# A decode kernel on one core: both FFN layers moved ahead of the attention heads, sums stacked, two engines' loops rolled, the last loads cut finer

## Chip, cores, metric

One core of one Trainium2 chip. The metric is the device time of one execution in microseconds (us), the median of the fast runs. "Span" is the length of the profiled execution as the trace shows it; the measured time of the same execution is 2.0 to 2.4 us longer.

## The reference

One decode step for two batch rows. x is 2x1x512, the caches are 2x32x8192x128 each, all bf16:

```python
xn = layernorm(x)                                     # over 512
q  = (xn @ wq) -> 2 x 32 heads x 128                  # wq 512 x 4096
p  = softmax(q . k_cache * 128**-0.5)                 # 8192 keys a head
o  = (p . v_cache) @ wo                               # wo 4096 x 512
h  = relu(xn @ w1)                                    # w1 512 x 1792
return x + o + h @ w2                                 # w2 1792 x 512
```

K and V are 268 MB of the 280.5 MB read, so this is a streaming kernel: every byte is used once.

## The kernel before

One engine (sync) issues all large loads into one queue. K and V are double buffered in 4.19 MB slots, one slot for one pair of heads (32 pairs). For each pair, TensorE (PE) transposes K in 16 groups of 8, VectorE (DVE) and ScalarE (ACT) copy the groups out of PSUM, PE makes scores, DVE takes the maximum, ACT the exponentials, and PE sums V of the pair before. The order of the loads, and what each waits for:

```python
nc.sync.dma_start(vs[1][:], wq).then_inc(dV[1], 16)      # wq borrows a V slot
block = nc.Block(no_gpsimd_drain=True)                   # (a barrier at its exit)
@block.sync
def _(sp):
    load_k(0); load_k(1); load_v(0)
    for t in range(NP - 1):
        if t + R < NP:
            sp.wait_ge(pT, NG * (t + 1))   # the transposes of pair t are done
            load_k(t + R)
        sp.wait_ge(sW, t + 1)              # the V sums of pair t-1 are done
        load_v(t + 1)
    # x8 (x again), w1, w2, then wo in three cuts (16, 12 and 4 of 32)
    sp.wait_ge(sE, 1)
    sp.dma_start(out, osb).then_inc(dO, 16)
# ... (cut)
block.__exit__(None, None, None)
nc.sync.wait_ge(dO, 16)
```

PE is rolled (a loop of 16 passes, two pairs each); DVE and ACT are straight code of 32 steps. q is 128 small matmuls of 2 columns; FFN1 and FFN2 (56 each) and the output projection (128) come in PE's tail, after the last V:

```python
for h in range(H):
    for kt in range(KT):
        pe.matmul(qp[:, h, :], lhsT=wq_sb[:, kt, h*Dh:(h+1)*Dh], rhs=xnT[:, kt, :], ...)
# ... 16 passes over the pairs, then the last V sums ...
ffn(0, FT // 2)                            # waits for w1
# ... OTn transposes, ffn(FT // 2, FT), selection ...
project(w2_sb, hT, 0, FT, first=True)      # waits for w2
for c in range(3):
    pe.wait_ge(dW[2 + c], 16)              # waits for each cut of wo
    t = project(wo_sb, OX, cuts[c], cuts[c + 1], last=(c == 2))
# then DVE adds x, PE transposes, DVE copies, sync stores
```

## Time and profile before

| | before |
|---|---|
| time, 3 runs | 662.76 us (662.54 to 662.95) |
| span | 660.4 us |
| bytes read | 280.50 MB, mean 425 GB/s |
| last load: first engine done / all 16 done | 652.8 / 656.2 us |
| store issued | 657.6 us |
| store landed, to the end of the span | 1.6 us |

How to read it: the loads are one stream through 16 DMA engines, and a load counts as landed when the last of its 16 has signalled. So the time has four terms: when the first engine is through with all bytes, how far the last engine lies behind it (the *spread*, or lateness), what the compute engines still do after the last landing, and the closing. The prediction shows the lines.

### The profile page before, as it was taken

To read this page: it belongs to the slowest core of one execution; us is meant where nothing else is said; L and a number is where in the kernel's file an instruction comes from. 1 tells how busy PE (TensorE), PEld (TensorE's weight loads), DVE (VectorE), ACT (ScalarE), POOL (GpSimd) and SP (SyncE) were. 2 spreads that over 40 slices of the span, in tenths; PEclk is the share of its full clock that TensorE was granted. 3 is DMA by queue.
4 is the path that set the end of the run, shared out by engine and by line. 5 is a ranking of instruction groups with operands and counts; after the bars stand their busy time and mean duration, and the time that the engine had idled before them with its cause. 6 is when DMAs were issued, how large, how long until landed. Compare 5 with 4: busy or idle time off the path is not lost.

```text
span 660.4 us, 26876 instructions
## 1 busy us (share of the span) xinstructions
PE 551.0 (83%) x12864; PEld 537.0 (81%) x12864; DVE 251.4 (38%) x433; ACT 236.7 (36%) x389; POOL 8.5 (1%) x44
## 2 busy tenths in 40 slices
PE   2577999898887889788798987887997878987976
PEld 2577999888887889788798887887987878987875
DVE  1233544344343434434344443343443433443411
ACT  1242444343433334333243343333343333343410
POOL 1000000000000000000000000000000000000000
PEclk9999999998898999889899898899898989997985
DMA  9999999999999999999999999999999999999995
GB/s 381 416 438 429 424 439 427 437 427 431 437 429 437 427 431 433 429 437 429 431 435 427 439 429 431 435 427 439 427 431 433 429 439 425 435 433 429 437 417 246
DMA packets 10133, 280.73 MB, mean 425 GB/s; under 512 B 1154, under 2 KB 1156, under 8 KB 1284
## 3 DMA queue, kind: packets, MB, share of 16 engines
q1 hardware_dynamic: 10112, 280.50, 98.9%
q8 instruction: 10, 0.16, 0.1%
q14 instruction: 7, 0.06, 0.0%
q10 hardware_dynamic: 4, 0.00, 0.0%
HBM read 280.50 MB, written 0.00 MB: 425 GB/s over the span
## 4 chain that ended last, share of the span: by engine, by line
DMA 62%; PE 34%; ACT 1%; issue 1%; SPq 0%; DVE 0%
DMA ks<-in_A_k_cache_dram 56%; PE tp L233 21%; PE Sc L240 10%; DMA wo_sb<-in_A_wo_dram 5%; PE ot L253 3%; ACT kT L380 1%; PE ot L356 0%; PE Sc L288 0%; PE Sc L291 0%; SPq L171 0%; SPq L168 0%; SPq L166 0%; SPq L149 0%; SPq L167 0%; SPq L147 0%
## 5 line engine op out<-in xcount | busy, mean ns | idle before, releaser
L233 PE MATMUL tp<-identb,ks 128*128 128x128 bf16 x4096 | 324.9, 229 | 77.8 <-DMA ks<-in_A_k_cache_dram 75.9
L380 DVE COPY kT<-tp 128x1024 bf16<-128x1024 bf16 x320 | 219.7, 691 | 332.9 <-PE tp L233 332.7
L233 PEld LDWEIGHTS tp<-identb,ks 128*128 128x128 bf16 x4096 | 256.1, 103 | 81.3 <-DMA ks<-in_A_k_cache_dram 79.1
L380 ACT COPY kT<-tp 128x1024 bf16<-128x1024 bf16 x192 | 194.3, 1012 | 249.6 <-PE tp L233 249.6
L240 PE MATMUL Sc<-q,kT 128*128 128x64 bf16 x4096 | 216.3, 196 | 3.4 <-ACT kT L380 3.4
L240 PEld LDWEIGHTS Sc<-q,kT 128*128 128x128 bf16 x4096 | 178.4, 100 | 6.7 <-ACT kT L380 6.7
L253 PE MATMUL ot<-prm,vs 128*128 128x64 bf16 x4224 | 157.6, 193 | 8.5 <-issue 5.0
L253 PEld LDWEIGHTS ot<-prm,vs 128*128 128x128 bf16 x4224 | 140.5, 98 | 11.4 <-issue 8.8
L483 ACT COPY nm<-Sc 128x2 f32<-128x2 f32 x32 | 5.1, 160 | 118.2 <-PE Sc L291 118.2
L487 ACT ACTIVATE prm<-Sc,nm 64x128 bf16<-64x128 f32 x64 | 25.8, 402 | 1.4
L425 DVE TENSOR_REDUCE mcol<-Sc 64x1 bf16<-64x128 f32 x64 | 18.6, 291 | 17.6 <-PE Sc L240 17.2
L473 ACT COPY OTf<-ot 128x2 f32<-128x2 f32 x33 | 5.3, 160 | 35.3 <-PE ot L253 35.3
L430 DVE TENSOR_REDUCE mx<-Sc 1x2 bf16<-1x128 bf16 x32 | 8.9, 279 | 16.9 <-PE Sc L288 16.9
L203 POOL COPY q<-qb 128x2 bf16<-128x2 bf16 x32 | 5.8, 184 | 582.3 <-PE Sc L240 568.6
L487 ACT ACTIVATION_READ_ACCUMULATOR prm<-Sc,nm 64x1 f32 x64 | 11.8, 185 | 0.0
L218 PE MATMUL ot<-xnT,vs 128*128 128x2 bf16 x128 | 3.6, 165 | 8.3 <-DMA vs<-in_A_wq_dram 8.3
L218 PEld LDWEIGHTS ot<-xnT,vs 128*128 128x128 bf16 x128 | 3.5, 104 | 8.4 <-issue 8.4
L288 PE MATMUL Sc<-identb,mcol 128*1 128x128 bf16 x32 | 7.0, 217 | 0.0
L356 PE MATMUL ot<-OX,wo_sb 128*128 128x2 bf16 x128 | 3.7, 166 | 3.1 <-DMA wo_sb<-in_A_wo_dram 3.1
L356 PEld LDWEIGHTS ot<-OX,wo_sb 128*128 128x128 bf16 x128 | 3.6, 104 | 3.3 <-DMA wo_sb<-in_A_wo_dram 1.9
L291 PE MATMUL Sc<-mx,onesb 1*128 1x2 bf16 x32 | 5.5, 172 | 0.0
L436 DVE CAST xT<-tp 128x8 f32<-128x8 bf16 x1 | 0.2, 166 | 12.5 <-PE Sc L327 12.5
(49 smaller groups left out, 29.4 us busy)
## 6 DMA issues: line engine op xcount, KB each, us to landing
ks<-in_A_k_cache_dram SPq DMA_DIRECT2D x32, 4096.0 KB, 26.8
vs<-in_A_v_cache_dram SPq DMA_DIRECT2D x32, 4096.0 KB, 31.6
vs<-in_A_wq_dram SPq DMA_DIRECT2D x1, 4096.0 KB, 12.2
w_sb<-in_B_w_dram SPq DMA_DIRECT2D x2, 1792.0 KB, 25.9
wo_sb<-in_A_wo_dram SPq DMA_DIRECT2D x1, 2048.0 KB, 32.3
wo_sb<-in_A_wo_dram SPq DMA_DIRECT2D x1, 1536.0 KB, 35.5
wo_sb<-in_A_wo_dram SPq DMA_DIRECT2D x1, 512.0 KB, 36.3
xsb<-in_A_x_dram ACTq DMA_DIRECT2D x1, 2.0 KB
```

The costliest lines, as they stand in the source:

```text
L203: g.tensor_copy(q2[t % R][:], qb[:, 2 * t:2 * t + 2]).then_inc(sQ1, 1)
L218: i = pe.matmul(qp[:, h, :], lhsT=wq_sb[:, kt, h * Dh:(h + 1) * Dh], rhs=xnT[:, kt, :], start=(kt == 0), stop=(kt == KT - 1),)
L233: t = pe.transpose(tp[e % 4][:, i, :], ks[r][:, kk * Dh:(kk + 1) * Dh], identb[:])
L240: t = pe.matmul(Sc[r][:, 2 * kk:2 * kk + 2 * REP], lhsT=kT[e % 4][:, i, :], rhs=rep(q2[r][:]), start=True, stop=True,)
L253: t = pe.matmul(ot[r][:, 0:2 * REP], lhsT=vs[r][:, kk * Dh:(kk + 1) * Dh], rhs=rep(prm[r][:, kk, :]), start=(kk == 0), stop=(kk == KB - 1),)
L288: pe.transpose(tr_of(r), mcol[r][:], identb[:]).then_inc(sT, 1)
L291: pe.matmul(bc_of(r), lhsT=onesb[:], rhs=mx[r][:], start=True, stop=True).then_inc(sB, 1)
L356: t = pe.matmul(fin[:, c, :], lhsT=w[:, j, c * P:(c + 1) * P], rhs=act[:, j, :], start=(first and j == j0 and c == 0), stop=(last and j == ...
L380: fn(kT[e % 4][:], tp[e % 4][:]).then_inc(kR[e], 1)
L425: m = v.tensor_reduce(out=mcol[i][half, :], in_=S_of(i)[half, :, u], axis=AX.X, op=ALU.max)
L430: v.tensor_reduce(out=mx[i][:], in_=tr_of(i).rearrange("o (u m) -> o u m", u=2), axis=AX.X, op=ALU.max, negate=True,).then_inc(sX, 1)
L487: x = a.activation(out=prm[i][half, :, u], in_=S_of(i)[half, :, u], func=ACTF.Exp, bias=nm[i][half, u:u + 1], scale=1.0, accum_out=RS[half ...
```

## The change

Intent: leave nothing but wo behind the last V, make the tail of PE short, take away the instruction fetches that disturb the loads, and shorten the closing. The bytes stay the same but for a second read of x (2 KB), which is dropped. The diff, cut to its core:

```diff
@@ buffers: w1 and w2 lie where wo lies later
-    wo_sb = sb([P, WJ, D], bf16, "wo_sb")
-    w1_sb = sb([P, KT, Dff], bf16, "w1_sb")
-    w2_sb = sb([P, FT, D], bf16, "w2_sb")
+    w_sb = sb([P, max(WJ * D, KT * Dff + FT * D)], bf16, "w_sb")
+    w1_sb = w_sb[:, 0:KT * Dff].rearrange("p (kt f) -> p kt f", kt=KT)
+    w2_sb = w_sb[:, KT * Dff:KT * Dff + FT * D].rearrange("p (j n) -> p j n", j=FT)
+    wo_sb = w_sb[:, 0:WJ * D].rearrange("p (j n) -> p j n", j=WJ)
-    cuts = (0, 16, 28, WJ)
+    cuts = (0, 14, 21, 27, 30, WJ)
@@ order of the loads
+    nc.sync.dma_start(w1_sb, B_w1.rearrange("(p kt) f -> p kt f", kt=KT)).then_inc(dW1, 16)
     nc.sync.dma_start(vs[1][:], A_wq.rearrange("(p kt) n -> p (kt n)", kt=KT)).then_inc(dV[1], 16)
-    block = nc.Block(no_gpsimd_drain=True)
-    block.__enter__()
-    @block.sync
+    @(lambda f: f(nc.sync))
     def _(sp):
+        sp.dma_start(w2_sb, B_w2.rearrange("(p j) n -> p j n", j=FT)).then_inc(dW2, 16)
         load_k(0)
         ... (cut: the same loop, with a semaphore pT[e] for each group e)
+        for i in range(2):
+            sl = slice(i * SLOT // 2, (i + 1) * SLOT // 2)
+            sp.dma_start(
+                vs[(NP - 1) % R][:, sl], V_all[(NP - 1) * P:NP * P, sl]
+            ).then_inc(dH[i], 16)
         ... (cut: wo by cuts, then the store)
@@ gpsimd, at its end
+        g.wait_ge(dO, 16)
+        g.nop()
@@ tensor: FFN1 (and q alike, 32 of 512 columns) as stacked sums
+        w1_v = w1_sb.rearrange("p kt (f j) -> p kt j f", j=FT)
+        for g in range(FG):
+            nj = min(4, FT - 4 * g)
+            for kt in range(KT):
+                i = pe.matmul(
+                    hp[:, 0:nj * P].rearrange("c (l f) -> c l f", f=P),
+                    lhsT=xz[:, kt, Z - g * Bsz:Z - g * Bsz + FG * Bsz],
+                    rhs=w1_v[:, kt, 4 * g:4 * g + nj, :],
         ... (cut: transposes of h and q, FFN2 as 14 matmuls of 512 columns)
@@ tensor, tail: x and FFN2 enter the final sum early, then the last V by halves, then wo
+        for i in range(2):
+            pe.wait_ge(dH[i], 16)
+            for e in range(i * NG // 2, (i + 1) * NG // 2):
+                weighted(1, e)
@@ vector and scalar: loops in place of 32 straight steps
+        with v.Fori(0, NP // R):
+            for r in range(R):
+                v.reg_add(reg, reg, 1)
+                pair(r, reg)
+        with a.Fori(0, NP // R) as tr:
+            for r in range(R):
+                a.reg_add(reg, reg, 1)
+                pair(r, reg, tr * R + r)
-    block.__exit__(None, None, None)
-    nc.sync.wait_ge(dO, 16)
```

In a stacked sum, x stands in one of several column pairs of a matrix that is zero elsewhere (xz). So a group of 512 weight columns lands in its own two rows of one PSUM tile, and the weights stream through as the moving operand.

## The prediction

> **What bounds the kernel now.** I read the page's slices first, then the DMA part, the sync engine's waits, the windows at the end, and the timeline of both ends.
>
> The slices: are the loads ever idle?
>
> ```profile
> DMA  9999999999999999999999999999999999999995
> GB/s 381 416 438 429 424 439 427 437 427 431 437 429 437 427 431 433 429 437 429 431 435 427 439 429 431 435 427 439 427 431 433 429 439 425 435 433 429 437 417 246
> HBM read 280.50 MB, written 0.00 MB: 425 GB/s over the span
> PE 551.0 (83%) x12864; PEld 537.0 (81%) x12864; DVE 251.4 (38%) x433; ACT 236.7 (36%) x389; POOL 8.5 (1%) x44
> ```
>
> The reader is to see that the 16 DMA engines are full from slice 1 to slice 38 and PE is not. The completion records of the trace say it more sharply: after 84 us the 4.19 MB loads of K and V complete every 9.71 us, so 431.7 GB/s. The change moves the same 280.5 MB (it drops a 2 KB second read of x), so 280.5 MB / 431.7 GB/s = 649.8 us stay. Only what lies before the first byte, after the last byte, or between the engines can be won.
>
> The windows of the last 10 us (columns: window, length, busy us of PE, weight loads, DVE, ACT, POOL; clock, DMA share, GB/s):
>
> ```profile
> 650.00:652.00 2.00, 0.72 (x27) 0.75 (x28) 0.00 (x0) 0.00 (x0) 0.00 (x0) 0.50 0.99 414
> 652.00:654.00 2.00, 1.13 (x43) 1.04 (x40) 0.00 (x0) 0.00 (x0) 0.00 (x0) 0.50 0.69 274
> 654.00:656.00 2.00, 1.04 (x39) 1.04 (x40) 0.00 (x0) 0.00 (x0) 0.00 (x0) 0.50 0.13 51
> 656.00:657.00 1.00, 0.83 (x32) 0.74 (x28) 0.13 (x1) 0.00 (x0) 0.00 (x0) 0.50 0.06 16
> ```
>
> From 652 to 656 the share falls from 0.99 to 0.13: some engines are finished and a few are not. A load counts as landed when the slowest of its 16 engines has added its increment. In the completion records first and last increment of one load are 0.42 us apart for wq, 1.78 for K0, 1.88 at 84 us (seven engines late), 2.18 at 298 us, 3.23 at 464 us, and **3.39 us for the last piece of wo** (first engine 652.8, last 656.2). A late engine stays late, since it never has an idle moment. What makes it late are instruction fetches:
>
> ```profile
> q1 hardware_dynamic: 10112, 280.50, 98.9%
> q8 instruction: 10, 0.16, 0.1%
> q14 instruction: 7, 0.06, 0.0%
> ```
>
> The packet records place the q8 fetches (16,384 bytes, about 1.05 us) seven times between 20 and 69 us, in PE's first loop pass, then at 644.1, 652.5 and 656.6, in its tail code. Within the loads, q14 fetches of 8,192 bytes come at 78.5, 89.2, 259, 288, 452 and 501 us, when only DVE and ACT run straight code. Each of PE's seven puts another engine back by about 1.4 us; the one at 452 us hits an engine 2.2 us late and makes it 3.2 us late.
>
> The end of the timeline:
>
> ```profile
> 654.96 1.86 PE L356 MATMUL ot<-OX,wo_sb 128*128 128x2 bf16 x64 [1.83 <-DMA wo_sb<-in_A_wo_dram]
> 656.87 0.17 DVE L453 TENSOR_TENSOR yT<-ot,xT 128x8 bf16<-128x8 f32 x1 [8.25 <-PE ot L356]
> 657.09 0.27 PE L374 MATMUL tp<-identb,yT 128*8 128x128 bf16 x1 [0.26 <-DVE yT L453]
> 657.39 0.21 DVE L460 COPY osb<-tp 8x128 bf16<-8x128 bf16 x1 [0.36 <-PE tp L374]
> 657.63 0.32 SPq L173 DMA_DIRECT2D out_dram<-osb  x1
> ```
>
> The last byte lands at 656.2, the last 16 projections end at 656.84, the store is issued at 657.63 and complete at about 658.9; 1.5 us of closing barriers end the span at 660.4. The measured 662.76 lies 2.4 us above the span, which I keep.
>
> **What the Trainium skill says.** First, "Runtime: NRT & Kernel Launch", Instruction fetch mechanics: instructions are refilled in 16 KiB blocks of 256, PE holds 2,048 of them, and crossing a block is "mostly hidden". The trace agrees on the block (16,384 bytes, PE) and on the loop: 2 x (384 matmul and weight-load pairs) + small change = about 1,540 instructions are fetched once and not again for 570 us. On DVE and ACT the records show 8,192-byte pieces. Hidden it is not here: full DMA engines turn each fetch into lateness. Second, "DMA: Bandwidth & Descriptors", Why a DMA increments its semaphore by 16 and not by 1: one increment from each engine, only the full 16 means landed; the records show just that. Third, the same page, Where 436 GB/s comes from: 435 GB/s is the ceiling of the SBUF ports; 431.7 measured is 99% of it, so the middle of the kernel can't get faster. Fourth, "TensorE: Matmul & The Clock Gate", Wait — 56ns, not 53.3ns?: 512 columns take 426.7 ns cold and 215.7 ns warm. The trace has no 512-column matmul, but its 128-column transposes agree with the 107 and 56 ns of that place (24 in 2.74 us after an idle stretch, 8 in 0.45 us later).
>
> **The change part by part.**
>
> *FFN ahead of the heads.* 3.67 MB of w1 and w2 move from the end to the front, 3.67 / 0.4317 = 8.5 us. K0 lands 8.5 us later and the load of wo ends where it did: by itself nothing. PE must be ready with q when K0 lands. Before:
>
> ```profile
> 13.30 3.55 PE L218 MATMUL ot<-xnT,vs 128*128 128x2 bf16 x128 [8.33 <-DMA vs<-in_A_wq_dram]
> 24.27 2.74 PE L233 MATMUL tp<-identb,ks 128*128 128x128 bf16 x24 [7.43 <-DMA ks<-in_A_k_cache_dram]
> ```
>
> After: w1 lands at 13.2 - 9.7 + 4.3 = 7.8, wq at 17.5, w2 at 21.7, K0 at 31.4 to 32.8. FFN1 is 16 matmuls (about 14 of 512 columns): 14 x 0.427 = 6 us cold, and its strided read might double that (strided weight loads of w1 started every 65 ns, plain ones every 29): done at 14 to 20. q is 32 x 512 columns: some 9 cold and the rest warm, 9 x 0.427 + 23 x 0.216 = 8.8 us, or 13.7 all cold: done at 26.3 to 31, to 33 in the worst case. Copies and transposes 1.5 us, FFN2 14 x 0.216 = 3 us. PE is ready at about 31, in the expected case when K0 lands, at worst some 4 to 5 us late.
>
> What lateness costs is in the sync engine's waits: K(t+2) is issued when the transposes of t are done.
>
> ```profile
> SPq L144 <- PE tp L233: 423.9, 30, 33.6
> SPq L147 <- PE ot L253: 169.8, 31, 21.4
> ```
>
> Margins from issue times against when the first engine runs dry: K2 issued 36.5, needed 41.9; V1 44.5 against 51.6; K3 57.4 against 61.4; V2 65.0 against 71; K4 75.8 against 80.8. The least is **4.0 us**, and it grows, since a PE step takes 15.9 us where its loads take 19.4. All shift together by 8.5 us, so up to 4 us late costs nothing.
>
> *Stacked sums.* 128 + 56 + 56 small matmul pairs become 32 + 16 + 14. Off the path both before and after, but the PE tail loses 224 instructions (about 550 are left of some 780): one fetch less there.
>
> *Rolled DVE and ACT.* The six q14 fetches inside the loads vanish. Then each engine has at most one PE fetch, and the spread at the end stays where it was at 84 us, 1.9 us, in place of 3.39: **-1.5 us** at the last landing. Register waits may cost some 0.1 us each (a guess, nothing in the trace has DVE's); 16 of them a step is 1.6 us against 3.5 us of slack.
>
> *Last V in halves.* After the second half 64 sums at 43 ns (5.53 us / 128, tail) = 2.8 us, then OTn, transposes, Ob, sel, OX about 2 us (643.35 to 648.6 before, less the FFN matmuls between): OX is ready 4.9 us after V, 128 projections at 29 ns take 3.7 us, done 8.6 us after V. wo needs 4.19 / 0.4317 = 9.7 us. So PE waits on wo, as before.
>
> *wo in five cuts.* After the last landing 8 projections in place of 16, at 27 ns: -0.2 us. More and smaller packets: 16 more for each engine, 8 more for V, some 4 ns each (4,096-byte packets start every 155.5 ns, by size they'd need 151.7): +0.1 us.
>
> *GpSimd awaits the store, no block.* The block's barrier (done at 658.5) lay beside the store. After the store sync woke the others and collected four signals in turn, about 0.5 us of the 1.5. With the barrier's collector, GpSimd, waiting itself, I take **-0.3 us**.
>
> Sum: 662.8 - 1.5 - 0.2 + 0.1 - 0.3 = 660.9.
>
> **The rivals.** (1) *The 8.5 us at the end are work that now vanishes*: to be believed if the chain, which ends in the load of wo, hid idle loads. The share of 0.99 up to 652 speaks against it. It would give 654. (2) *The head starves the loads*: FFN1's stride and a cold clock make PE more than 4 us late, or register waits slow the first steps; the K3 margin is broken and 1 to 4 us of load time are lost. For it: the margin is thin and no trace row has such a matmul. It would give 662 to 665. (3) *The spread does not shrink*: a tail fetch hits an engine that is already late, so 3.0 in place of 1.9. For it: at 652.5 just this happened, 2.1 became 3.3. Against: PE's fetches took seven different engines in turn, and the engine hit then had been made late by q14. It would give 662.0.
>
> **Range and chances.** Floor: no spread at all is 662.8 - 3.4 - 0.4 = 659.0. Rival 3 gives 662.0, a mild rival 2 about 662.5. So 659.8 to 662.5 holds it 8 times in 10. 2% is 13 us; no part is that large in either direction: faster 0.01, same 0.98, slower 0.01.
>
> **What would show it.** Right: DMA share 0.9 or more through slices 1 to 38 at 425 to 439 GB/s; q14 packets inside the loads gone; first to last increment of the final wo piece about 1.9 us; last landing about 654.8; store issued 1.2 us after it; closing part about 1.2 us. Wrong: a window before 100 us with DMA share under 0.9 (rival 2), a spread over 2.5 us (rival 3), or a projection group that starts after its wo piece landed, which would mean that PE, not the load, ends the kernel.

## The result, and the profile after

Ratios are the mean time of one kernel's fast runs over that of the other's of the same rounds, so not quite the ratio of the medians quoted.

| | before | after |
|---|---|---|
| time | 662.73 (662.54 to 662.95) | **661.66** (661.42 to 661.82) |
| ratio | | 0.9984 (95%: 0.9971 to 0.9996), "same" |
| span | 660.45 | 659.72 |
| first engine through with all bytes | 652.77 | 652.98 |
| spread of the last piece of wo | 3.39 | 2.88 |
| last landing | 656.16 | 655.86 |
| from it to the issue of the store | 1.48 | 1.22 |
| store landed to end of span | 1.62 | 1.44 |
| profiled run's time minus its span | 2.35 | 2.03 |

Six runs each. The landings come from the completion records of the trace, where each engine's increment has its own time. The differences, +0.21 (first engine), -0.51 (spread), -0.26, -0.18 and -0.32, add up to -1.06 us; the medians differ by -1.07. So it is small change in five places, in a kernel whose middle did not move.

The slices and the busy times of the page after:

```profile
DMA  8999999999999999999999999999999999999996
GB/s 360 431 437 432 424 435 425 441 429 429 435 427 439 425 435 431 431 433 425 441 425 433 437 425 439 425 435 431 431 433 425 441 427 431 437 425 439 425 424 259
PE 568.2 (86%) x12701; PEld 535.8 (81%) x12701; DVE 253.6 (38%) x437; ACT 255.8 (39%) x403; POOL 8.8 (1%) x46
```

Slices 1 to 38 are full, as before: 163 matmuls fewer (12864 to 12701) changed nothing in them. The queues of the page after (packets, MB, share):

```profile
q1 hardware_dynamic: 10528, 280.50, 99.0%
q8 instruction: 9, 0.15, 0.1%
q14 instruction: 1, 0.01, 0.0%
```

The six q14 fetches inside the loads are gone; the packet records put the remaining one at 658.6, after the store. Of PE's nine, six still lie in the first loop pass (37.2 to 70.8 us) and three at the end (646.6, 652.7, 656.2). The end of the timeline after, PE's last projections to the store:

```profile
655.28 1.00 PE L410 MATMUL ot<-OX,w_sb 128*128 128x2 bf16 x20 [0.16 <-DMA w_sb<-in_A_wo_dram]
656.32 0.17 DVE L517 CAST yT<-ot 128x8 bf16<-128x8 f32 x1 [4.91 <-PE ot L410]
656.84 0.21 DVE L519 COPY osb<-tp 8x128 bf16<-8x128 bf16 x1 [0.36 <-PE tp L419]
657.08 0.37 SPq L194 DMA_DIRECT2D out_dram<-osb  x1
```

The bracket of the first row says that PE still waits for wo ("<-DMA"); the store is issued at 657.08 in place of 657.63. The windows of that stretch (columns as in the prediction):

```profile
652.00:654.00 2.00, 1.82 (x69) 1.73 (x65) 0.00 (x0) 0.00 (x0) 0.00 (x0) 0.50 0.69 265
654.00:656.00 2.00, 1.38 (x39) 1.22 (x40) 0.00 (x0) 0.00 (x0) 0.00 (x0) 0.50 0.16 56
656.00:657.00 1.00, 0.55 (x9) 0.28 (x9) 0.32 (x2) 0.00 (x0) 0.00 (x0) 0.50 0.06 16
```

The DMA shares (0.69, 0.16) are nearly those of before (0.69, 0.13). So some engines are again through with their work up to 2.9 us before the last one is: the spread that was to shrink to 1.9 us is 2.88.

The head of PE's timeline after: FFN1, q, and the first transposes of K0:

```profile
8.84 12.92 PE L249 MATMUL ot<-w_sb,xz 128*8 128x512 bf16 x16 [3.03 <-DMA w_sb<-in_B_w_dram]
21.58 8.23 PE L260 MATMUL ot<-vs,xz 128*16 128x512 bf16 x32
33.88 1.51 PE L298 MATMUL tp<-identb,ks 128*128 128x128 bf16 x24
```

FFN1 took 12.92 us. Four of its 16 matmuls are half as wide, so these are 14 full ones of 0.92 us; PE reached K0 at 33.9, 1.5 us after it had landed (32.4).

### The profile page after: what moved, and what is told of

It is laid out like the page before. It is cut to its first block, busy times and chain, and to the rows that moved or that the text cites. A ratio compares the mean times of both kernels' runs of the same rounds, so it can differ in the third digit from the quotient of the medians.

```text
span 659.7 us, 26788 instructions
## 1 busy us (share of the span) xinstructions
PE 568.2 (86%) x12701; PEld 535.8 (81%) x12701; DVE 253.6 (38%) x437; ACT 255.8 (39%) x403; POOL 8.8 (1%) x46
## 4 chain that ended last, share of the span: by engine, by line
DMA 59%; PE 37%; ACT 2%; issue 1%; SPq 0%; DVE 0%; ACTq 0%
DMA ks<-in_A_k_cache_dram 53%; PE tp L298 20%; PE Sc L305 10%; DMA w_sb<-in_A_wo_dram 4%; PE ot L318 3%; PE ot L249 2%; ACT kT L425 2%; PE ot L260 1%; DMA w_sb<-in_B_w_dram 1%; PE Sc L283 0%; ACT L425 0%; SPq L192 0%; SPq L187 0%; PE Sc L353 0%; DVE qs L459 0%
## 5 line engine op out<-in xcount | busy, mean ns | idle before, releaser
L249 PE MATMUL ot<-w_sb,xz 128*8 128x512 bf16 (+1 forms) x16 | 12.9, 975 | 3.0 <-DMA w_sb<-in_B_w_dram 3.0
L532 ACT COPY OTf<-ot 128x2 f32 x32 | 5.1, 160 | 22.4 <-PE ot L318 22.4
L249 PEld LDWEIGHTS ot<-w_sb,xz 128*8 128x8 bf16 x16 | 1.6, 104 | 13.4 <-issue 13.4
L544 ACT ACTIVATION_READ_ACCUMULATOR prm<-Sc,nm x64 | 11.8, 185 | 0.0
L260 PE MATMUL ot<-vs,xz 128*16 128x512 bf16 x32 | 8.2, 422 | 0.0
L260 PEld LDWEIGHTS ot<-vs,xz 128*16 128x16 bf16 x32 | 3.1, 98 | 5.4 <-issue 2.4
```

The source lines that it names most:

```text
L249: i = pe.matmul(hp[:, 0:nj * P].rearrange("c (l f) -> c l f", f=P), lhsT=xz[:, kt, Z - g * Bsz:Z - g * Bsz + FG * Bsz], rhs=w1_v[:, kt, 4 ...
L260: i = pe.matmul(qp, lhsT=xz[:, kt, Z - g * Bsz:Z - g * Bsz + QG * Bsz], rhs=vs[1][:, (kt * QG + g) * 512:(kt * QG + g + 1) * 512], start=( ...
L532: a.copy(OTf[:, bass.ds(c, 2)], ot[r][:, 0:2]).then_inc(sO, 1)
L544: x = a.activation(out=prm[i][half, :, u], in_=S_of(i)[half, :, u], func=ACTF.Exp, bias=nm[i][half, u:u + 1], scale=1.0, accum_out=RS[half ...
```

## The experiments

**Theory (uneven engines):** the time is the bytes, plus the spread, plus a fixed ending. The spread shrank by only 0.5 us because something other than the DVE and ACT fetches makes engines late. **Rivals:** (a) it is the order of the loads or FFN1's slow read at the head that costs; (b) the rolled loops gave the gain and something else took it back; (c) the halves of V or the finer cuts bought the 1.1 us; (d) it is the closing alone. All twelve runs had five rounds, in three groups of four; the kernels of a group shared a chip and the runs of the kernel before (medians 663.09, 662.86, 662.78). One run of before in the first group took 1951.72 us, counts as slow and is left out.

### Group 1

**DVE and ACT straight again** (a_straight):

```diff
-        with v.Fori(0, NP // R):
-            for r in range(R):
-                v.reg_add(reg, reg, 1)
-                pair(r, reg)
+        for t in range(NP):
+            pair(t % R, t + 1)
   (ACT alike)
```

> The changed kernel with DVE and ACT written out again, nothing else undone. Theory (lateness of DMA engines by instruction fetches): six fetches of 8,192 bytes come back between 70 and 510 us, at least one of them on an engine that is already late, so the spread between first and last increment of the final wo piece goes from 2.9 to 3.3 - 4.3 us and the time from 661.7 to 662.1 - 663. The 16 ACT table loads in the loop vanish. Rival (rolling changed nothing for the loads, the spread of 2.9 is set by the start alone): spread 2.9 and time 661.7, give or take 0.2. Second rival (the reloads of the ACT table in the rolled loop cost time): faster, below 661.3.

Measured: 661.92 us (661.81 to 662.38), ratio 0.9982 (0.9968 to 0.9996). The queue line of its page:

```profile
q14 instruction: 7, 0.06, 0.0%
```

The six fetches are back, at 76.7, 94.8, 254.9, 294.6, 450.2 and 510.2 us. The spread is 2.98 against 2.88, below the 3.3 expected, and the time the same within the intervals; it isn't faster either, so the table loads cost nothing that shows. So the fetches, which I had made the main item, are worth some 0.1 to 0.3 us in this kernel: the engines they hit were not the last one. The spread was 2.75 before the fetch at 450 and 3.08 after it, since that fetch made an engine that was 2.07 us late 3.08 us late.

**Before, with only the loops rolled** (b_rolled): the kernel before, its Block kept, DVE and ACT as in the change.

```diff
-    pT, sS, sT, sB, sW = sem("pT"), ...
+    pT = [sem(f"pT{e}") for e in range(NG)]
-        for t in range(NP):                      # DVE; ACT alike
-            ...
+        with v.Fori(0, NP // R):
+            for r in range(R):
+                v.reg_add(reg, reg, 1)
+                pair(r, reg)
```

> The kernel before with DVE and ACT rolled, nothing else changed: its first load is still wq with 32 KB packets. Theory: no 8,192-byte fetches within the loads; the first load is landed within 0.4 us, every engine takes at most one fetch of PE, so the spread at the end is 1.9 us in place of 3.39 and the time 662.7 - 1.5 = 661.2. Rival (PE's fetches hit late engines anyway, as in the changed kernel): spread 2.9 or more, time 662.2 or more.

Measured: 662.91 us (662.66 to 663.35), ratio 0.9995 (0.9981 to 1.0009): no gain that the interval shows.

```profile
q8 instruction: 10, 0.16, 0.1%
q14 instruction: 1, 0.01, 0.0%
```

This run is the prediction's step in isolation, and it shows both halves of it. Without q14 fetches the spread held at 2.05 to 2.12 us from the landing at 92.8 us to that at 650.3, near what I had reckoned (1.9). Then PE's tail fetch at 651.1 hit an engine that was already 1.4 us late, and the spread ended at 2.94. That is the prediction's third rival, in the kernel where the rest of the argument held.

**wq first, FFN1 read in runs of four** (a_wq_first):

```diff
-    w1 load; wq load
+    wq load; w1 load                       # and q's sums ahead of FFN1 on PE and DVE
-                    hp[:, 0:nj * P].rearrange("c (l f) -> c l f", f=P),
-                    rhs=w1_v[:, kt, 4 * g:4 * g + nj, :],
+                    hp.rearrange("c (f l) -> c f l", l=4)[:, :, 0:nj],
+                    rhs=w1_v[:, kt, :, 4 * g:4 * g + nj],      # w1_v as "p kt f j"
```

> The changed kernel with wq loaded ahead of w1, q summed ahead of FFN1 and FFN1 reading runs of four columns. Theory (the changed kernel's spread of 2.9 is the 1.47 us unevenness of its first load, w1 in 14,336-byte packets, plus one PE fetch of 1.4): first load landed within 0.5 us, final spread 1.9 - 2.1 us, time 660.7 - 660.9. Rival (unevenness comes from the position of the fetches, not from the first load): final spread 2.5 - 3, time 661.6. FFN1's matmuls should take 0.43 us or less in place of 0.91, PE be ready near 31 us and K2 be issued no later than 45 us.

Measured: **661.11 us (661.08 to 661.35), ratio 0.9968 (0.9954 to 0.9982)**. Head and end of PE's timeline:

```profile
13.29 9.32 PE L247 MATMUL ot<-vs,xz 128*16 128x512 bf16 x32 [8.66 <-DMA vs<-in_A_wq_dram]
22.44 4.47 PE L261 MATMUL ot<-w_sb,xz 128*8 128x512 bf16 x16
...
655.47 0.40 PE L412 MATMUL ot<-OX,w_sb 128*128 128x2 bf16 x9 [0.74 <-issue]
```

FFN1 takes 4.47 us in place of 12.92, and PE now waits for K0 (its first transpose starts at 31.47). But that is not where the time came from (see a_fast_ffn1 below). The first load's own spread is 0.41 us in place of 1.47, and the last one's is 1.83: what the first load leaves uneven, the later ones inherit. The last landing comes at 654.86, 1.0 us earlier. Of this 0.6 us is not cashed: the last row waits for "issue", which is to say for nothing the profile shows. By the instruction records PE stood 0.9 us (from one start to the next) at the 25th from its end, and the store was issued 1.82 us after the landing instead of 1.22.

**The last V whole** (a_v_whole):

```diff
-        for i in range(2): ... two loads, dH[0] and dH[1]
+        sp.dma_start(vs[(NP - 1) % R][:], V_all[(NP - 1) * P:NP * P, :]).then_inc(dH[0], 16)
-            pe.wait_ge(dH[i], 16)
+            pe.wait_ge(dH[0], 16)
```

> The changed kernel with the last V in one load. Theory (the halves are needed because nothing but wo follows V): all 128 sums start only when V has landed at 645.9, so 5.5 + 1.5 + 3.8 us later, at 656.7 or after, PE ends, 0.4 - 0.6 us later than the 656.3 of the changed kernel; time 662.1 - 662.3, and the last wo piece is no longer waited for. Rival (PE's tail is hidden by wo in either case): time 661.7.

Measured: 661.75 us (661.4 to 662.1), ratio 0.9977 (0.9963 to 0.9992).

```profile
645.59 5.54 PE L314 MATMUL ot<-prm,vs 128*128 128x64 bf16 x128 [0.42 <-DMA vs<-in_A_v_cache_dram]
652.64 3.35 PE L406 MATMUL ot<-OX,w_sb 128*128 128x2 bf16 x128 [0.32 <-DVE OX L509]
656.75 0.37 SPq L190 DMA_DIRECT2D out_dram<-osb  x1
```

PE is late here: the projections start only when OX is ready, run at one go (26 ns each) and end at 656.0, half a microsecond after the last landing (655.50), which is where they would have ended anyway. The theory that the halves are needed fell: they cost and bring nothing that can be measured.

### Group 2

**The change unaltered** (a_again), as the yardstick of this group.

> The changed kernel itself once more, as a yardstick on the same chip for the other three: 661.4 - 662.0, spread between first and last increment of the final wo piece 2.7 - 3.0 us, span 2.0 us below the measured time.

Measured: 661.77 us (661.51 to 661.95), ratio 0.9983 (0.9969 to 0.9997). First engine 652.77, spread 2.87, last landing 655.64, closing 1.44: the same terms as the first time, so they belong to the kernel and not to one execution.

**wq first, with 228 empty instructions at PE's start** (a_wq_first_pad), to shift PE's block edges off the tail:

```diff
+        for _ in range(228):
+            pe.nop()
         pe.wait_ge(sI, 1)
```

> wq first, as before, and 228 empty PE instructions ahead of the program, which PE passes while it waits for its first load. Theory: in a_wq_first PE stood for 0.9 us at the 25th instruction from its end, which lies on a 256-instruction block, since a block needs some 6 us from the crossing of the one before; the padding puts that block's edge behind the last projection. Then the last projections end 0.25 us after the last landing, the store is issued 1.2 us after it in place of 1.8, time 660.4 - 660.6. Rival (the stand of 0.9 us is not a matter of the block's edge): a stand of the same length at the same place, time 661.1.

Measured: 661.10 us (660.84 to 661.15), ratio 0.9972 (0.9958 to 0.9986). As a test it failed: the trace has as many PE records as without them (25,546), and PE stood again, 0.66 us, at the 25th from the end. The empty instructions left no sign in the trace, so the run says nothing of block edges. It does repeat a_wq_first: 0.67 us better than the unaltered change of its own group.

**Sync waits for the store in place of GpSimd** (a_sync_waits):

```diff
         ).then_inc(dO, 16)
+        sp.wait_ge(dO, 16)
...
-        g.wait_ge(dO, 16)
-        g.nop()
```

> The changed kernel, but sync waits for the store and not GpSimd. Theory (prediction): the closing part from the landing of the store to the end of the span grows from 1.44 to 1.6 - 1.75 us and the time by 0.2 - 0.3 us over a_again. What lies between span and measured time (2.0 us, 2.4 in the kernel before) stays at 2.0 if the missing block is its cause, and goes to 2.4 if it is GpSimd's wait.

Measured: 662.15 us (662.13 to 662.59), ratio 0.9991 (0.9978 to 1.0005). From the store's landing to the end of the span it takes 2.00 us in place of 1.44, with the same time outside the span (2.02). So *who* waits is worth 0.56 us of closing, more than expected, and 0.4 us of time; and the time outside the span doesn't depend on it.

**No load of w2** (a_no_w2), wrong (relative error 1.37): FFN2 reads w1's bytes.

```diff
-    w2_sb = w_sb[:, KT * Dff:KT * Dff + FT * D].rearrange(...)
+    w2_sb = w_sb[:, 0:FT * D].rearrange(...)
-        sp.dma_start(w2_sb, ...).then_inc(dW2, 16)
-        pe.wait_ge(dW2, 16)
+        pe.wait_ge(dW1, 16)
```

> Wrong on purpose: w2 isn't loaded, FFN2 reads w1's bytes in its place, so 1.835 MB less are moved and all instructions stay. Theory (bytes alone set the middle): 1.835 MB / 431.7 GB/s = 4.25 us less than a_again, 657.4, with the same 9.71 us between the landings of K and V. Rival (the head binds, PE is late with q and the loads wait for it): less than 3 us are won, and a DMA share under 0.9 shows before 70 us.

Measured: 658.69 us (657.32 to 659.6), ratio 0.9929 (0.9915 to 0.9943). By the rate, the 1.84 MB are worth 1.84 / 0.4317 = 4.25 us. The fastest run gains 4.19 over the fastest of the unaltered change in its group (661.51), so bytes are the currency. But the medians differ by only 3.1, short of what I expected: the runs lie 2.3 us apart, and the profiled one gained only 2.2 on the median of 661.77. In it the loads ran dry. Where the sync engine issues K2, in this kernel:

```profile
45.22 0.33 SPq L163 DMA_DIRECT2D ks<-in_A_k_cache_dram  x1
```

and the windows behind it:

```profile
44.00:46.00 2.00, 2.00 (x58) 2.00 (x55) 1.38 (x2) 0.85 (x1) 0.00 (x0) 1.00 0.77 320
47.00:48.00 1.00, 0.88 (x29) 0.88 (x30) 0.05 (x1) 0.00 (x0) 0.00 (x0) 1.00 0.26 98
```

The same windows of the change, whose K2 was issued at 44.82:

```profile
44.00:46.00 2.00, 2.00 (x59) 1.93 (x56) 1.38 (x2) 0.46 (x1) 0.00 (x0) 1.00 0.92 385
47.00:48.00 1.00, 1.00 (x31) 0.88 (x28) 0.21 (x1) 0.00 (x0) 0.00 (x0) 1.00 1.06 459
```

Without w2 the first engine is through with all that was queued at 45.98; K2 was issued 0.76 us before that, and the first completion of K2 came 10.90 us after that of the load before in place of 9.71, so 1.19 us were lost. K3 was issued 0.97 us before the first engine was dry, and 0.96 were lost. So in this kernel a load has to be issued some 1.9 us (0.76 + 1.19, 0.97 + 0.96) before the engines run dry. In the change K2 and K3 had 5.6 and 4.6 us, so its head starves nothing, but the real slack is 2.6 us and not 4.6. This is the prediction's second rival, one small step away.

### Group 3

**wq first, with 114 real transposes at PE's start** (a_wq_first_fill), to shift the edges by 228 instructions that the trace does see:

```diff
+        for _ in range(114):
+            pe.transpose(tp[3][:, 0, :], identb[:], identb[:])
         pe.wait_ge(sV, 6)
```

> wq first, and 114 throwaway transposes (228 PE instructions) while PE waits for wq, since the empty instructions of the padded try left no trace and moved nothing. Theory: the stand of PE at the 25th instruction from its end is the edge of a 256-instruction block; moved by 228 that edge lies behind the last projection, a stand appears at the 253rd from the end at most. Last projections 0.4 - 0.5 us after the last landing, store issued 1.2 - 1.3 us after it, time 660.5 - 660.7 where a_wq_first had 661.1. Warm PE: q's 32 sums in about 7 us in place of 9.3. Rival (the stand is not the block's edge): again 0.5 - 0.9 us at the 25th, time 661.1.

Measured: 662.23 us (660.96 to 662.78), ratio 0.999 (0.9976 to 1.0003). The end of its timeline:

```profile
655.95 1.00 PE L414 MATMUL ot<-OX,w_sb 128*128 128x2 bf16 x20 [1.69 <-DMA w_sb<-in_A_wo_dram]
657.75 0.37 SPq L195 DMA_DIRECT2D out_dram<-osb  x1
```

With 228 PE records more, the stand at the 25th from the end is gone. That alone doesn't test the edge, since PE came there late, 2.7 us after the last fetch began. What speaks for the edge are the instruction records of all the runs. In the first loop pass PE stands at instructions 256 apart, and each of these stands ends 2.3 to 2.6 us after a PE fetch began. In a_wq_first, its padded form and a_wq_halves PE stands at the 281st and the 25th from its end, 256 apart, and there too until 2.3 to 2.6 us after a fetch. The change (after) came to its 25th 2.9 us after the fetch and did not stand. The shift also brought a further PE fetch (14.0 us) and moved the others, and the last, at 653.6, hit an engine 2.1 us late: the spread went from 2.10 to 3.6 us there, and PE waits 1.69 us for wo. One of five runs escaped (660.96; no trace was kept of it). The edit deals the fetches anew; it isn't a repair.

**wq first, loaded in two halves** (a_wq_halves):

```diff
-    nc.sync.dma_start(vs[1][:], wq_v).then_inc(dV[1], 16)
+    nc.sync.dma_start(vs[1][:, 0:SLOT // 2], wq_v[:, 0:SLOT // 2]).then_inc(dQ, 16)
+    nc.sync.dma_start(vs[1][:, SLOT // 2:SLOT], wq_v[:, SLOT // 2:SLOT]).then_inc(dV[1], 16)
```

> wq first, but in two loads of 16,384-byte packets. Theory (short packets at the very start leave the engines uneven): first load 0.8 - 1.5 us from first to last increment, final spread 2.5 - 3.0, time 661.4 - 661.7. Rival (it is w1's layout or place, not the packet size): first load within 0.5 us, final spread 1.8 - 1.9, time 661.1.

Measured: 661.16 us (661.02 to 661.29), ratio 0.9976 (0.9962 to 0.9990). The spread of the first load is 0.41 us, the last one's 1.86. I had suspected the size of the first load's packets; this fell. Why w1 in front leaves the engines 1.1 to 1.5 us apart and wq 0.4 to 0.75 stays open.

**Before, without the Block, GpSimd waiting** (b_noblock):

```diff
-    block = nc.Block(no_gpsimd_drain=True)
-    block.__enter__()
-    block.__exit__(None, None, None)
-    nc.sync.wait_ge(dO, 16)
+        g.wait_ge(dO, 16)                  # at the end of GpSimd's code
+        g.nop()
```

> The kernel before without its block, GpSimd waiting for the store, all else as it was. Theory: the closing part falls from 1.62 to 1.44 us and what lies between span and measured time from 2.4 to 2.0, so 662.3 where before has 662.8; spread at the end 3.0 - 3.4 as before. Rival (the 0.4 outside the span comes from the rolled engines or from FFN's place): it stays at 2.4 and the time is 662.6.

Measured: 662.07 us (661.99 to 662.61), ratio 0.9993 (0.9979 to 1.0006). By the medians -0.7 us; the interval reaches zero. The trace says where it would be: closing 1.31 in place of 1.62, and the time outside the span 2.05 in place of 2.35. In the profiled runs, all eleven kernels without the Block have 2.02 to 2.05 there; the two with it, before and b_rolled, have 2.35 and 2.43. Its spread, 3.30, is that of before.

**The change with only FFN1's read altered** (a_fast_ffn1): the rhs and output views of a_wq_first, w1 still first.

> The changed kernel, FFN1 reading runs of four columns, w1 still first. Theory: FFN1's 16 matmuls take 0.43 us cold and 0.28 warm in place of 0.91, PE is ready with q and y by about 31, some 2 to 3 us sooner, and the time stays (661.5 - 661.8), because PE's lateness of 1.5 us was inside the 4 us of slack; first load still spread by 1.3 - 1.5 us and the end by 2.7 - 3.0. Rival (the late head costs time): 0.5 us or more faster.

Measured: 661.41 us (661.36 to 661.91), ratio 0.9982 (0.9968 to 0.9996), that of the unaltered change.

```profile
8.39 6.17 PE L250 MATMUL ot<-w_sb,xz 128*8 128x512 bf16 x16 [3.75 <-DMA w_sb<-in_B_w_dram]
32.02 1.51 PE L300 MATMUL tp<-identb,ks 128*128 128x128 bf16 x24
```

FFN1 is halved and PE is at K0 1.9 us earlier, and no time came of it that the intervals show: the head is off the path. What a_wq_first gained it owes to the order of the loads, with which PE's order (q before FFN1) changed too. Within this group that order is worth 0.25 us (661.16 for a_wq_halves against 661.41); between the groups it looks like 0.6. The Trainium skill's "SBUF — State Buffer", Door 1: The DMA port swizzle, says that SBUF has cachelines of 16 bytes, that a line needs at least two hits for full bandwidth, and that each access which crosses to a new line pays. The runs agree: columns 28 bytes apart took 0.92 us for 512, runs of four (8 bytes) 6.17 / 14 = 0.44 when PE had just been idle, and 4.47 / 14 = 0.32 right behind the sums of q (a_wq_first).

## Why the prediction was right, and where its steps were not

The prediction said 660.9 (659.8 to 662.5) and "same"; 661.66 lies inside. Its steps:

- **The bytes bound it, and work moved from the tail brings nothing by itself: right.** Slices full, 9.71 us a load, the first engine through within 0.2 us of before. The first rival (654) is refuted, and a_no_w2 shows what does count: 4.19 us for 1.84 MB, fastest run against fastest.
- **"The spread at the end stays where it was at 84 us, 1.9 us: -1.5 us": the step that failed.** It measured -0.51. The prediction's own sign of being wrong, a spread over 2.5 us, came true (2.88), and 661.66 lies nearer to the 662.0 that it gave for a spread that doesn't shrink than to its 660.9. The removal of the fetches was right and is seen; its size was not. I took before's starting spread (0.42) as given and reckoned with at most one fetch per engine. With w1 in front the first load left 1.47. Then PE's first loop pass added its fetches as before. Two of them (64.5 and 70.8 us) fell between the landings at 62.3 and 72.9. Sorted, the 16 increments of these two loads show one engine going from on time to 1.5 us late, and one of those that the first load had left about 1.4 us late going to 3.1; the one that was 2.1 us late stayed there. With wq first all six fetches hit engines at most 0.4 us late, and the spread stayed at 1.9. So the change was at its end value within a ninth of its time, and fetches that are removed later count only if they would have made another engine the slowest. a_straight (+0.1 to 0.3), b_rolled (2.1 held until 650) and a_wq_first (1.83 with a good start) show the three parts one by one. Which engine a fetch hits I can't predict.
- **The third rival** (a tail fetch on a late engine) happened, but can't be seen in the spread: the tail fetch at 646.6 made an engine that was 1.4 us late 2.97 us late, beside the slowest one's 2.96. By itself it was enough for the final spread. In b_rolled and a_wq_first_fill such a fetch did set it.
- **Cuts of wo, -0.2: right** (1.48 to 1.22 from landing to store; no run undid the cuts alone).
- **Closing, -0.3: mechanism right, size short.** -0.18 within the span (-0.31 in b_noblock), and -0.32 outside of it, which I had assumed fixed at 2.4. a_sync_waits ties 0.56 us of closing to GpSimd's wait; it and b_noblock together tie the part outside the span to the Block.
- **PE ready at about 31, "might double": worse than that.** 0.92 us a matmul where 0.85 was my worst case, ready at 33.9. It cost nothing (a_fast_ffn1), as the prediction's slack said; yet that slack was read 2 us too generously (a_no_w2).
- **"PE waits on wo, as before", with the halves: right, but the halves aren't the reason** (a_v_whole).
- **Readings that don't hold, and on which little rests:** the fetch in before's tail at 652.5 made an engine 3.3 us late that was 1.9 late, not 2.1; 3.23 is the spread at 453.1 us, not 464; and PE's tail has three fetches as before (two in a_again), not one less.
- **Not foreseen:** the rolled ACT loop reloads its function table in every pass. From the costliest groups of the page after:

```profile
L425 ACT ACT_TABLE_LOAD x16 | 20.5, 1283 | 2.2
```

16 times 1.28 us where the code of before has two in all. ACT is busy 39%, and the loads did not run dry for it.

So the total came out within 0.8 us partly by luck, because errors of opposite sign met: 1.0 us too much hoped for from the spread (1.5 less 0.51) and 0.1 each from the first engine and the closing, against 0.32 not counted on from outside the span. A version with a better result exists: a_wq_first, 661.1, beats both; its code ran in two further forms (a_wq_first_pad, a_wq_halves) at 661.10 and 661.16.

## What to carry to other kernels

When one stream of loads fills all DMA engines, look past the mean rate: read the first and the last increment of each load, from the first load on, for in these runs an engine that fell behind early stayed behind to the end. Test what a removed disturbance is worth by the slowest engine, not by their number: six fetches went away and the end moved little. And put numbers on slack with a run that uses it up: here a load had to be issued about 2 us before the engines ran dry, not at the moment they did.

## What the Trainium skill lacked or had wrong

- "Runtime: NRT & Kernel Launch", Instruction fetch mechanics, calls the crossing of a block "mostly hidden". With the DMA engines full it is not: each PE fetch of 16,384 bytes took about 1.05 us and left its engine 1.4 to 1.7 us late for the rest of the kernel. PE itself stood 0.6 to 2.9 us at points 256 instructions apart in the first loop pass of before and after, and 0.9 us at the tail of a_wq_first, until some 2.5 us after the fetch began.
- No page that I read says how far the engines drift apart within an uninterrupted stream: 0.42 us at the first load, 3.39 at the last in the kernel before. Nor that it depends on which load goes first (wq 0.4 to 0.75, w1 1.1 to 1.5); the cause of that is open.
- "DMA: Bandwidth & Descriptors", Specifications, gives about 0.6 us to the first byte for loads issued by sync or scalar. That is not the lead that a load needs to keep the engines full: issued 0.76 and 0.97 us before they ran dry (a_no_w2), loads still lost 1.19 and 0.96 us, so some 1.9 us were needed.
- No page that I read says that the closing depends on which engine waits for the last store: it took 1.44 us from landing to the end when GpSimd waited for it, 2.00 when sync did.
